# Expert layers of a routed MLP: two 64-token groups per step, one in each half of the array's columns, with both weight matrices streamed

## The chip, the cores and the metric

One core of one Trainium2 chip. The metric is device time in microseconds (us) of one execution, as the median of several runs. The profile and the trace are of one further execution of the same program, recorded by the hardware profiler.

## What is computed

Attention in chunks of 64 positions over 8 batches, 8 heads, 576 positions and head size 64. Its output, as 4608 tokens of 512 numbers, goes through 8 experts; each token goes to the one expert whose embedding is nearest by cosine.

```python
scores = scale * q_c @ k_c.T            # within each chunk of 64
x = softmax(scores) @ v_c               # -> (4608, 512)
logits = xn @ en.T / tau                # rows and expert embeddings normed
expert_idx = argmax(logits, axis=1)
out[mask] = gate_w[mask, None] * (relu(x[mask] @ w1[e]) @ w2[e])   # for each expert e
```

w1 is (8, 512, 1024) and w2 (8, 1024, 512), all in 32-bit floats. The inputs are drawn with a fixed seed, so the number of tokens of each expert can be worked out from the reference: 832, 359, 183, 448, 512, 1023, 576 and 675.

## The kernel before

It has three stages, and the order of all work is as written in the code (`manual_schedule`): each engine and each DMA queue takes its instructions in that order and waits where it must.

**Attention** (lines 88 to 267) goes through 36 tiles of 128 tokens. `load_qk` (L90) and `load_v` (L104) put the loads of q, k and v on SyncE's queue (SP), q and k three tiles ahead. Per tile, TensorE transposes k and q (`turn_qk`, L126), multiplies them in quarters of the array (`scores`, L144: 64 rows by 64 columns, four neighbours in the loop `for par: for c:` lie in four different quarters, and the two values of `c` lie in the same rows and in different columns), transposes the weights (L171) and multiplies by v, again in quarters (`values`, L184). `turn_x` (L208) and `logits` (L216) make the router's logits. The tile's rows go to DRAM on GpSimd's queue (L199). Beside it `load_w1` (L115) puts one piece of 512 KB of w1 per tile on SP, 32 pieces, so that all of w1 (16 MB) lies in `w1_sb` when the experts begin.

**Routing** (lines 279 to 432) is a chain of small VectorE operations: the best expert of each token, the token's rank among its expert's tokens, the number of blocks of each expert (L349), the first block of each (L352), the expert of each block (`eblk`, L358 to L366) and whether it differs from that two blocks before (`fresh`, L367, L368), each token's block and row (L380 to L382), its gate, and the token at each place by one-hot products (L404 to L430).

**Experts** (lines 437 to 566): 43 blocks of 128 tokens of one expert, the most that 4608 tokens and 8 experts can need. A block is gathered from DRAM by an indirect DMA on GpSimd (`gather`, L469, four ahead), transposed (`turn_xb`, L483), multiplied by w1 (`hidden`, L495), transposed again (`turn_h`, L516), multiplied by w2 (`result`, L527) and scattered (L536). `load_w2` (L459) puts a load of 2 MB into one of two buffers; it is skipped where that buffer holds the expert already. SP and TensorE read the block's expert into a register first (`number`, L450). A matrix product of 32-bit floats shows as two instructions, with a weight load before each, so `hidden` and `result` have 16 each. The loop runs, for step j:

```python
hidden(j + 1); turn_h(j); turn_xb(j + 2); result(j - 1); load_w2(j + 1); gather(j + XBUF)
```

Of the kernel before, what the change touches and what calls it, by code (L numbers as in the profile page):

```python
# [9 lines left out]
FP32 = mybir.dt.float32  # L10
# [8 lines left out]
P = 128  # L19
CH = 64  # L20
ROUND = 12582912.0  # 1.5 * 2**23: adding and subtracting it rounds to a whole number
# [4 lines left out]
def kernel(  # L26
# [17 lines left out]
    KD = D // P  # 128-row pieces of the model dimension  # L44
    KF = F // P  # 128-row pieces of the hidden dimension
    NT = N // P  # tiles of 128 tokens
    NCB = S // CH  # chunks in a batch
    NBLK = NT + E - 1  # blocks of 128 tokens of one expert, at most
# [6 lines left out]

    w1_sb = keep.tile([P, E, KD, F], FP32, name="w1_sb")
    w1_flat = w1_sb.rearrange("p e c f -> p (e c f)")
# [3 lines left out]
    src_row = keep.tile([P, NBLK], I32, name="src_row")  # L61
    dst_row = keep.tile([P, NBLK], I32, name="dst_row")
    gate_at = keep.tile([P, NBLK], FP32, name="gate_at")
    eblk = keep.tile([1, NBLK], I32, name="eblk")
    fresh = keep.tile([1, NBLK], I32, name="fresh")

    make_identity(nc, ident)

    # ------------------------------------------------------------------
    # chunk attention: x rows to DRAM, logits and squared norms on chip  # L70
    # ------------------------------------------------------------------
    with (
# [31 lines left out]
        def load_v(b):  # L104
            # odd heads' keys in the upper half, where their transposed weights come out
            t = v_p.tile([P, NPAIR, NCB, Dh], FP32, tag="v", name="v")
            for h in range(H):
                r0 = CH * (h % 2)
                nc.sync.dma_start(
                    out=t[r0 : r0 + CH, h // 2],  # L110
                    in_=v[b, h].rearrange("(c k) d -> k c d", k=CH),
                )
            v_t[b] = t

        def load_w1(j):  # L115
            e, c = divmod(j, KD)
            nc.sync.dma_start(out=w1_sb[:, e, c], in_=moe_w1[e, c * P : c * P + P])
# [106 lines left out]
        def set_up_experts():  # L224
            # rows of emb / (norm + 1e-6) / tau, turned
            junk = one.tile([P, D], FP32, tag="junk", name="junk")
            nc.scalar.activation(junk[0:E], emb, AF.Square, accum_out=emb_sq)
            nc.scalar.activation(emb_n, emb_sq, AF.Sqrt)
            nc.vector.tensor_scalar(emb_n, emb_n, 1e-6, None, ALU.add)
            nc.vector.reciprocal(emb_n, emb_n)  # L230
            nc.vector.reciprocal(tau_sb, tau_sb)
            nc.vector.tensor_scalar(emb, emb, emb_n, tau_sb, ALU.mult, ALU.mult)
            ps = ps_t.tile([P, KD, P], FP32, tag="tr", name="tr")
            for c in range(KD):
                nc.tensor.transpose(ps[:, c, 0:E], emb[:, c * P : c * P + P], ident[0:E, 0:E])
            nc.vector.tensor_copy(enT, ps[:, :, 0:E])
# [11 lines left out]
        for t in range(NT + 1):  # L248
            if t < NT:
                turn_a(t)  # L250
            if t + 1 < NT:
                turn_qk(t + 1)
                scores(t + 1)
            if t > 0:
                turn_x(t - 1)
            if t < NT:
                values(t)
                if t + 4 < NT:
                    load_qk(t + 4)
                b = (2 * t + 2) // NCB + 1  # L260
                if b not in v_t and b < B:
                    load_v(b)
                if 1 <= t <= KD * E:
                    load_w1(t - 1)
            if t > 0:
                logits(t - 1)
        nc.vector.tensor_copy(lg, lg_ps)

    # ------------------------------------------------------------------
    # routing: the best expert and its gate for each token, and a place for  # L270
    # each token among blocks of 128 that belong to one expert each
    # (counts and 0/1 masks are whole numbers up to 128, exact in bf16)
    # ------------------------------------------------------------------
    with (
# [42 lines left out]
        # rank of each token among its expert's  # L317
# [26 lines left out]
        # blocks of each expert, and the first of them  # L344
# [3 lines left out]
        half = 0.5 - 0.5 / P  # L348
        nc.vector.tensor_scalar(nb, tot, 1.0 / P, half, ALU.mult, ALU.add)  # L349
        nc.vector.tensor_scalar(nb, nb, ROUND, ROUND, ALU.add, ALU.subtract)  # L350
        nc.vector.tensor_tensor_scan(first, carry[:, 0, 1 : E + 1], nb, 0.0, ALU.mult, ALU.add)
        nc.vector.tensor_tensor(first, first, nb, ALU.subtract)  # L352
        nc.vector.tensor_scalar(off, first, float(P), None, ALU.mult)

        # expert of each block, and whether its weights differ from those two blocks before
        e_of = sp.tile([1, NBLK], FP32, name="e_of")
        ge = sp.tile([1, NBLK, E], FP32, name="ge")
        nc.vector.tensor_tensor(  # L358
            ge,
            io[0:1, 0:NBLK].unsqueeze(2).to_broadcast([1, NBLK, E]),  # L360
            first[0:1].unsqueeze(1).to_broadcast([1, NBLK, E]),
            ALU.is_ge,
        )
        nc.vector.tensor_reduce(e_of, ge, axis=AX.X, op=ALU.add)
        nc.vector.tensor_scalar(e_of, e_of, -1.0, None, ALU.add)
        nc.vector.tensor_copy(eblk, e_of)  # L366
        nc.vector.memset(fresh[:, 0:2], 1)  # L367
        nc.vector.tensor_tensor(  # L368
            fresh[:, 2:NBLK], e_of[:, 2:NBLK], e_of[:, 0 : NBLK - 2], ALU.not_equal
        )  # L370

        # place of each token: block and row
# [7 lines left out]
        nc.vector.tensor_scalar(blk, dest, 1.0 / P, -half, ALU.mult, ALU.add)  # L380
        nc.vector.tensor_scalar(blk, blk, ROUND, ROUND, ALU.add, ALU.subtract)
        nc.vector.scalar_tensor_tensor(  # L382
            out=row, in0=blk, scalar=-float(P), in1=dest, op0=ALU.mult, op1=ALU.add
        )

        # gates
# [13 lines left out]
        # token and gate at each place: one-hot products  # L400
        SK = [P, NT, NBLK]
        bm = sp.tile(SK, FP32, name="bm")
        rr = sp.tile([P, NT, 2, NBLK], FP32, name="rr")
        nc.vector.tensor_tensor(  # L404
            bm,
            io[:, 0:NBLK].unsqueeze(1).to_broadcast(SK),
# [5 lines left out]
        inv = ps_r.tile([P, 2, NBLK], FP32, name="inv")  # L412
# [10 lines left out]
        # an empty place reads row 0 and writes nowhere  # L423
        bad = sp.tile([P, NBLK], FP32, name="bad")
        tk = sp.tile([P, NBLK], FP32, name="tk")
# [8 lines left out]
    # ------------------------------------------------------------------  # L434
    # experts, a block of 128 tokens at a time
    # ------------------------------------------------------------------
    XBUF = 4
    with (
        tc.tile_pool(name="w2", bufs=1) as w2_p,
# [6 lines left out]
        w2_sb = [w2_p.tile([P, KF, D], FP32, name=f"w2_{i}") for i in range(2)]  # L446
        w2_rows = moe_w2.rearrange("e (c p) d -> p (e c) d", p=P)
# [10 lines left out]

        def load_w2(j):  # L459
            e = number(eblk[0:1, j : j + 1], E - 1, ENG.SP)  # L460
            # skipped where this buffer holds that expert already
            how = {}
            if j >= 2:
                how["cond"] = number(fresh[0:1, j : j + 1], 1, ENG.SP) > 0
            nc.sync.dma_start(out=w2_sb[j % 2], in_=w2_rows[:, ds(e * KF, KF), :], **how)

# [21 lines left out]
        def hidden(j):  # L488
            d = mo[j]
            e = number(eblk[0:1, j : j + 1], E - 1, ENG.PE)  # L490
            h = bp.tile([P, F], FP32, tag="h", name="h")
            for fh in range(F // 512):
                ps = ps_h.tile([P, 512], FP32, tag="h", name="h_ps")
                for c in range(KD):
                    nc.tensor.matmul(  # L495
                        ps,
                        lhsT=d["xT"][:, c],
                        rhs=w1_flat[:, ds(e * (KD * F) + c * F + fh * 512, 512)],
                        start=(c == 0),
                        stop=(c == KD - 1),  # L500
                    )
# [21 lines left out]
        def result(j):  # L523
            d = mo.pop(j)
            ps = ps_y.tile([P, D], FP32, tag="y", name="y_ps")
            for c in range(KF):
                nc.tensor.matmul(  # L527
                    ps,
                    lhsT=d["hT"][:, c],
                    rhs=w2_sb[j % 2][:, c],  # L530
                    start=(c == 0),
                    stop=(c == KF - 1),
                )
# [12 lines left out]

        load_w2(0)
# [4 lines left out]
        hidden(0)  # L552
        turn_xb(1)
        for j in range(NBLK + 1):
            if j + 1 < NBLK:
                hidden(j + 1)
            if j < NBLK:
                turn_h(j)
            if j + 2 < NBLK:
                turn_xb(j + 2)  # L560
            if j > 0:
                result(j - 1)
                if j + 1 < NBLK:
                    load_w2(j + 1)
            if j + XBUF < NBLK:
                gather(j + XBUF)
# [28 lines left out]
```

## Time and profile before

| | before |
|---|---|
| median of 3 runs | 1083.26 us (1082.6 to 1084.11) |
| span of the profiled execution | 1082.1 us |
| TensorE busy, matrix products | 940.4 us (87%) |
| VectorE, ScalarE, GpSimd busy | 272.5, 178.6, 109.7 us |
| bytes moved by DMA | 109.65 MB |

The profiled execution has no other time of its own than its span, which is 1.2 us under the median. PE is TensorE's matrix products, PEld its weight loads (they run beside the products), DVE is VectorE, ACT ScalarE, POOL GpSimd, SP SyncE. Starts are recorded; the ends of matrix products are modelled, so the time from one start to the next says more than a duration. The granted clock of TensorE is given as a share of 2.4 GHz; its two levels are 0.5 (1.2 GHz) and 1.0.

### The profile page before, as it was taken

What the parts mean: (1) busy time and instruction counts of PE and PEld (TensorE: products, weight loads), DVE (VectorE), ACT (ScalarE), POOL (GpSimd) and SP (SyncE); (2) the same over time, 40 slices, a digit from 0 to 9 for tenths busy, and PEclk for the clock granted to TensorE, in tenths of its full rate; (3) what the DMA queues carried; (4) which work ended last, traced back from release to release, by engine and by line L of the source; (5) the groups of instructions that cost most, each with busy time, mean ns of one, the idle gap of its engine ahead of it and who ended that gap; (6) DMA issues with size and microseconds to landing.
All of it is one profiled execution on the core that took longest, in us unless ns stands there. A gap on an engine that the chain in (4) does not pass through costs nothing.

```text
span 1082.1 us, 12876 instructions
## 1 busy us (share of the span) xinstructions
PE 940.4 (87%) x5139; PEld 569.7 (53%) x5139; DVE 272.5 (25%) x506; ACT 178.6 (17%) x319; POOL 109.7 (10%) x134
## 2 busy tenths in 40 slices
PE   4777777777777736999999999999999999999998
PEld 3666566666666624444444444444444444444443
DVE  3434434434434382111111111111111111111110
ACT  3222222222222210111111111111111110111101
POOL 0000000000000001011101111011110111101101
PEclk9999655555555555999999999999999999999999
DMA  9574755737744105011143531415100331321100
GB/s 189 143 171 130 178 143 156 181 113 180 167 129 116 40 0 204 1 39 40 47 162 117 193 111 44 165 40 194 39 30 29 117 117 39 120 89 39 40 3 0
DMA packets 144026, 109.65 MB, mean 101 GB/s; under 512 B 116118, under 2 KB 116118, under 8 KB 143968
## 3 DMA queue, kind: packets, MB, share of 16 engines
q1 hardware_dynamic: 134144, 78.66, 27.7%
q0 software_dynamic: 9824, 30.17, 7.8%
q8 instruction: 42, 0.69, 0.3%
q14 instruction: 16, 0.13, 0.0%
HBM read 146.55 MB, written 20.71 MB: 155 GB/s over the span
## 4 chain that ended last, share of the span: by engine, by line
issue 56%; PE 20%; DVE 14%; POOL 5%; ACT 2%; DMA 1%; POOLq 0%; SPq 0%
PE lg_ps L216 6%; PE tr L126 6%; PE sc L144 4%; POOL xin L469 4%; PE tr L171 3%; DVE a L154 2%; DVE mx L152 2%; DVE qT L131 2%; DVE rs L162 2%; ACT a L160 2%; DVE xT L210 2%; POOL out_dram L536 2%; PE inv L416 1%; DMA xin<-x_rows,src_row 1%; DVE rs L163 1%
## 5 line engine op out<-in xcount | busy, mean ns | idle before, releaser
L495 PE MATMUL h_ps<-w_sb,xbT 128*128 x688 | 304.9, 596 | 2.4 <-DVE xbT L485 1.6
L527 PE MATMUL y_ps<-w,hT 128*128 128x512 f32 x688 | 302.2, 592 | 0.0
L495 PEld LDWEIGHTS h_ps<-w_sb,xbT 128*128 128x128 f32 x688 | 131.4, 191 | 167.7 <-issue 164.5
L527 PEld LDWEIGHTS y_ps<-w,hT 128*128 128x128 f32 x688 | 127.5, 190 | 144.4 <-issue 144.4
L506 DVE TENSOR_SCALAR h<-h_ps 128x512 f32<-128x512 f32 x43 | 29.7, 691 | 400.6 <-PE h_ps L495 400.6
L216 PE MATMUL lg_ps<-enT,xT 128*128 128x8 f32 x288 | 64.2, 352 | 62.1 <-DVE xT L210 62.1
L536 POOL DMA_INDIRECT out_dram<-y,dst_row x43 | 43.5, 1011 | 558.9 <-ACT y L535 544.7
L216 PEld LDWEIGHTS lg_ps<-enT,xT 128*128 128x128 f32 x288 | 60.8, 312 | 69.0 <-DVE xT L210 68.9
L535 ACT ACTIVATE y<-y_ps,gate_at 128x512 f32<-128x512 f32 x43 | 29.5, 687 | 285.8 <-PE y_ps L527 285.8
L504 ACT ACTIVATE h<-h_ps 128x512 f32<-128x512 f32 x43 | 25.7, 597 | 308.3 <-PE h_ps L495 308.3
L144 PE MATMUL sc<-kT,qT 64*64 64x64 f32 x1152 | 40.8, 317 | 31.5 <-DVE qT L131 31.5
L520 DVE COPY hT<-ht_ps 128x512 f32<-128x512 f32 x43 | 29.7, 691 | 140.4 <-PE ht_ps L516 140.4
L131 DVE COPY qT<-tr 128x512 f32<-128x512 f32 x36 | 24.9, 691 | 139.2 <-PE tr L126 139.2
L144 PEld LDWEIGHTS sc<-kT,qT 64*64 64x64 f32 x1152 | 35.1, 218 | 44.9 <-issue 41.1
L199 POOL DMA_DIRECT2D x_rows<-x x36 | 19.5, 542 | 353.6 <-DVE x L192 353.6
L516 PEld LDWEIGHTS ht_ps<-ident,h 128*128 128x128 f32 x344 | 40.3, 141 | 22.7 <-issue 22.7
L469 POOL DMA_INDIRECT xin<-x_rows,src_row x43 | 43.9, 1021 | 52.4 <-DVE dst_row L430 35.1
L516 PE MATMUL ht_ps<-ident,h 128*128 128x128 f32 x344 | 44.6, 273 | 0.0
L160 ACT ACTIVATE a<-a 128x512 f32<-128x512 f32 x36 | 22.7, 629 | 132.5 <-DVE a L154 132.5
L126 PE MATMUL tr<-ident,kx 128*128 128x128 f32 x144 | 36.9, 409 | 6.0 <-DMA kx<-in_k_dram 6.0
L184 PE MATMUL sc<-v,aT 64*64 64x64 f32 x1152 | 40.8, 318 | 0.2 <-ACT aT L173 0.2
L184 PEld LDWEIGHTS sc<-v,aT 64*64 64x64 f32 x1152 | 34.1, 218 | 11.8 <-issue 11.3
(108 smaller groups left out, 615.3 us busy)
## 6 DMA issues: line engine op xcount, KB each, us to landing
w<-in_moe_w_dram SPq DMA_DIRECT2D x43, 2048.0 KB
w_sb<-in_moe_w_dram SPq DMA_DIRECT2D x32, 512.0 KB
v<-in_v_dram SPq DMA_DIRECT2D x64, 144.0 KB
x_rows<-x POOLq DMA_DIRECT2D x36, 256.0 KB, 2.3
qx<-in_q_dram SPq DMA_DIRECT2D x32, 256.0 KB
kx<-in_k_dram SPq DMA_DIRECT2D x32, 256.0 KB
qx<-in_q_dram SPq DMA_DIRECT2D x8, 128.0 KB
kx<-in_k_dram SPq DMA_DIRECT2D x8, 128.0 KB
```

Source lines behind the costliest of these rows:

```text
L126: nc.tensor.transpose(ps[:, i], a[:, i * P : i * P + P], ident)
L131: nc.vector.tensor_copy(x, ps)
L144: nc.tensor.matmul(sc[CH * c : CH * c + CH, par, i], lhsT=qx[r0 : r0 + CH, i, c0 : c0 + CH], rhs=kx[r0 : r0 + CH, i, c0 : c0 + CH], start= ...
L160: nc.scalar.activation(a, a, AF.Exp, scale=scale)
L171: nc.tensor.transpose(ps[:, i], d["a"][:, i].rearrange("p r k -> p (r k)"), ident)
L184: nc.tensor.matmul(pv[CH * c : CH * c + CH, par, i], lhsT=d["aT"][r0 : r0 + CH, i, CH * c : CH * c + CH], rhs=v_t[b][r0 : r0 + CH, i, cb], ...
L216: nc.tensor.matmul(lg_ps[:, t], lhsT=d["xT"][:, c], rhs=enT[:, c], start=(c == 0), stop=(c == KD - 1),)
L469: nc.gpsimd.indirect_dma_start(out=t, out_offset=None, in_=x_rows, in_offset=bass.IndirectOffsetOnAxis(ap=src_row[:, j : j + 1], axis=0), ...
L495: nc.tensor.matmul(ps, lhsT=d["xT"][:, c], rhs=w1_flat[:, ds(e * (KD * F) + c * F + fh * 512, 512)], start=(c == 0), stop=(c == KD - 1),)
L516: nc.tensor.transpose(ps[:, c], d["h"][:, f0 : f0 + P], ident)
L527: nc.tensor.matmul(ps, lhsT=d["hT"][:, c], rhs=w2_sb[j % 2][:, c], start=(c == 0), stop=(c == KF - 1),)
L536: ins = nc.gpsimd.indirect_dma_start(out=out, out_offset=bass.IndirectOffsetOnAxis(ap=dst_row[:, j : j + 1], axis=0), in_=y, in_offset=Non ...
```

## The change

The experts' work is cut into groups of 64 tokens (G) instead of blocks of 128, and a step takes two groups: one from the front of the list of groups, in the lower 64 columns of the array, one from its back, in the upper 64. `NST` is 40 steps. The two groups of a step may belong to different experts, so each half has its own weights: two buffers of w1 and two of w2 per half, 2 MB each. w1 no longer stays on the chip whole. In attention, the buffers of the first two steps are filled with the first expert's weights (front) and the last one's (back), 8 loads of 2 MB at every fourth tile; during the experts, both w1 and w2 are loaded anew into a buffer whose expert changes. TensorE reads no register any more; SP reads two per half and step. The transposes stay as they were.

```diff
+    w1_sb = [[keep.tile([P, KD, F], FP32, name=f"w1_{s}{i}") for i in range(2)] for s in range(2)]
+    w2_sb = [[keep.tile([P, KF, D], FP32, name=f"w2_{s}{i}") for i in range(2)] for s in range(2)]
...
-                if 1 <= t <= KD * E:
-                    load_w1(t - 1)
+                if t % 4 == 3 and t // 4 < 8:
+                    load_first(t // 4)
...
-        nc.vector.tensor_scalar(nb, tot, 1.0 / P, half, ALU.mult, ALU.add)
+        nc.vector.tensor_scalar(nb, tot, 1.0 / G, half, ALU.mult, ALU.add)
+        nc.vector.tensor_scalar(ngm1, first[:, E - 1 : E], -1.0, None, ALU.add)
+        nc.vector.tensor_scalar(mid, first[:, E - 1 : E], 0.5, 0.25, ALU.mult, ALU.add)
+        nc.vector.tensor_scalar(mid, mid, ROUND, ROUND, ALU.add, ALU.subtract)
...
+        nc.vector.tensor_copy(jj[:, 0], io[0:1, 0:NST])
+        nc.vector.tensor_scalar(jj[:, 1], io[0:1, 0:NST], -1.0, ngm1[0:1], ALU.mult, ALU.add)
...
-        nc.vector.memset(fresh[:, 0:2], 1)
+        for i in range(2):
+            nc.vector.tensor_scalar(
+                fresh[:, i, 0:2], e_of[:, i, 0:2], float((0, E - 1)[i]), None, ALU.not_equal
+            )
...
+        nc.vector.tensor_scalar(back, blk, mid, None, ALU.is_ge)
+        nc.vector.scalar_tensor_tensor(
+            out=row, in0=back, scalar=float(G), in1=row, op0=ALU.mult, op1=ALU.add
+        )
+        nc.vector.tensor_scalar(turn, blk, -2.0, ngm1, ALU.mult, ALU.add)
+        nc.vector.tensor_tensor(turn, turn, back, ALU.mult)
+        nc.vector.tensor_tensor(blk, blk, turn, ALU.add)
...
+        def load_w(buf, rows, n, s, j):
+            if (s, j) not in new:
+                new[s, j] = (
+                    number(eblk[0:1, s, j : j + 1], E - 1, ENG.SP),
+                    number(fresh[0:1, s, j : j + 1], 1, ENG.SP),
+                )
+            e, f = new[s, j]
+            nc.sync.dma_start(out=buf[s][j % 2], in_=rows[:, ds(e * n, n), :], cond=f > 0)
...
                 for c in range(KD):
-                    nc.tensor.matmul(
-                        ps,
-                        lhsT=d["xT"][:, c],
-                        rhs=w1_flat[:, ds(e * (KD * F) + c * F + fh * 512, 512)],
...
+                    for s in range(2):
+                        nc.tensor.matmul(
+                            ps[G * s : G * s + G],
+                            lhsT=d["xT"][:, c, G * s : G * s + G],
+                            rhs=w1_sb[s][j % 2][:, c, fh * 512 : fh * 512 + 512],
...
+        load_w1(0)
+        load_w1(1)
         load_w2(0)
         load_w2(1)
...
-        for j in range(NBLK + 1):
-            if j + 1 < NBLK:
+        for j in range(NST + 1):
+            if j + 1 < NST:
                 hidden(j + 1)
+                if j + 3 < NST:
+                    load_w1(j + 3)
```

`result` is changed as `hidden` is, with `w2_sb[s][j % 2][:, c]`; `load_w1(j)` and `load_w2(j)` call `load_w` for both halves. Where both do their work, the order on SP in step j is `load_w1(j + 3)` and then `load_w2(j + 1)`.

## Rows read from the trace of the kernel before

**Rows 1.** Busy time by stage; columns: stretch, its length, then as headed.
```profile
core 0: us, PE busy (x) PEld busy (x) DVE busy (x) ACT busy (x) POOL busy (x), PEclk, DMA share, GB/s
0.00:380.00 380.00, 273.33 (x3172) 237.05 (x3172) 155.96 (x294) 95.14 (x187) 21.61 (x45) 0.67 0.60 145
380.00:424.30 44.30, 16.33 (x75) 15.67 (x75) 27.44 (x84) 3.08 (x4) 4.80 (x8) 0.50 0.16 56
424.30:1082.10 657.80, 650.73 (x1892) 316.94 (x1892) 89.12 (x129) 80.38 (x129) 83.27 (x82) 0.99 0.23 79
```

**Rows 2.** TensorE's own waits in the experts' stage; us in total, times, longest.
```profile
PE x_ps L483 <- DMA xin<-x_rows,src_row: 9.8, 1, 9.8
PE h_ps L495 <- DVE xbT L485: 1.6, 2, 0.8
PE h_ps L495 <- DMA w<-in_moe_w_dram: 0.8, 1, 0.8
```

**Rows 3.** Timeline of TensorE over one step; start, length, instructions (x count).
```profile
506.40 7.03 PE L495 MATMUL h_ps<-w_sb,xbT 128*128 x16
513.27 1.04 PE L516 MATMUL ht_ps<-ident,h 128*128 128x128 f32 x8
514.14 0.60 PE L483 MATMUL x_ps<-ident,xin 128*128 128x128 f32 x4
514.58 7.03 PE L527 MATMUL y_ps<-w,hT 128*128 128x512 f32 x16
521.45 0.59 PE L495 MATMUL h_ps<-w_sb,xbT 128*128 x1
```

**Rows 4.** Timeline of TensorE over part of one attention tile.
```profile
290.03 1.06 PE L126 MATMUL tr<-ident,kx 128*128 128x128 f32 x4
290.88 1.06 PE L126 MATMUL tr<-ident,qx 128*128 128x128 f32 x4
...
293.89 1.11 PE L208 MATMUL tr<-ident,x 128*128 128x128 f32 x4
294.93 0.39 PE L184 MATMUL sc<-v,aT 64*64 64x64 f32 x4
```

**Rows 5.** The same tile's scores, cut at 293.16 us.
```profile
292.82 0.60 PE L144 MATMUL sc<-kT,qT 64*64 64x64 f32 x12 [0.88 <-DVE qT L131]
```

**Rows 6.** Weight loads of both expert products, from the groups of instructions.
```profile
L495 PEld LDWEIGHTS h_ps<-w_sb,xbT 128*128 128x128 f32 x688 | 131.4, 191 | 167.7 <-issue 164.5
L527 PEld LDWEIGHTS y_ps<-w,hT 128*128 128x128 f32 x688 | 127.5, 190 | 144.4 <-issue 144.4
```

**Rows 7.** VectorE in the routing, groups of instructions.
```profile
L358 DVE TENSOR_TENSOR ge<-io,first 1x344 f32<-1x344 f32 x1 | 0.5, 496 | 0.0
L364 DVE TENSOR_REDUCE e_of<-ge 1x43 f32<-1x344 f32 x1 | 0.5, 499 | 0.0
L382 DVE SCALAR_TENSOR_TENSOR row<-blk,dest 128x36 f32<-128x36 f32 x1 | 0.2, 195 | 0.0
L353 DVE TENSOR_SCALAR off<-first 128x8 f32<-128x8 f32 x1 | 0.2, 172 | 0.0
```

**Rows 8.** The chain that ended last: start, length, what (the first gather).
```profile
415.87 8.34 DMA xin<-x_rows,src_row
```

**Rows 9.** DMA: issues, count, median us to landing; and SP's queue in bytes.
```profile
xin<-x_rows,src_row POOLq DMA_INDIRECT x43, 3.9
q1 hardware_dynamic: 134144, 78.66, 27.7%
```

**Rows 10.** Stretches with w2 loads; the last two columns are DMA share and GB/s.
```profile
416.60:432.00 15.40, 6.87 (x12) 3.27 (x13) 0.69 (x1) 0.00 (x0) 4.38 (x5) 0.54 0.97 351
583.00:592.00 9.00, 9.00 (x32) 4.65 (x31) 2.07 (x3) 1.18 (x2) 1.84 (x2) 1.00 0.88 289
```

**Rows 11.** SP's register reads, and its longest waits in the whole span and in attention.
```profile
L451 SPq TENSOR_LOAD <-fresh x41: 261/266/273, 417.3 to 1048.7; - x41
...
SPq L465 <- PE y_ps L527: 586.5, 41, 33.6
...
SPq L97 <- PE tr L126: 182.2, 24, 8.7
```

More of the change, by code (lines that the diff above doesn't have):

```diff
@@ L47 @@
     NCB = S // CH
-    NBLK = NT + E - 1
+    G = P // 2
+    NST = NT + E // 2
     scale = 1.0 / float(Dh) ** 0.5
@@ L54 @@
     ctx.enter_context(tc.manual_schedule())
-    w1_sb = keep.tile([P, E, KD, F], FP32, name="w1_sb")
-    w1_flat = w1_sb.rearrange("p e c f -> p (e c f)")
+    w1_sb = [[keep.tile([P, KD, F], FP32, name=f"w1_{s}{i}") for i in range(2)] for s in range(2)]
+    w2_sb = [[keep.tile([P, KF, D], FP32, name=f"w2_{s}{i}") for i in range(2)] for s in range(2)]
+    w1_rows = moe_w1.rearrange("e (c p) f -> p (e c) f", p=P)
+    w2_rows = moe_w2.rearrange("e (c p) d -> p (e c) d", p=P)
     ident = keep.tile([P, P], FP32, name="ident")
@@ L60 @@
     nsq = keep.tile([P, NT], FP32, name="nsq")
[L61 to L65, printed above, removed]
+    src_row = keep.tile([P, NST], I32, name="src_row")
+    dst_row = keep.tile([P, NST], I32, name="dst_row")
+    gate_at = keep.tile([P, NST], FP32, name="gate_at")
+    eblk = keep.tile([1, 2, NST], I32, name="eblk")
+    fresh = keep.tile([1, 2, NST], I32, name="fresh")
     make_identity(nc, ident)
@@ L113, in load_v, with load_first @@
             v_t[b] = t
-        def load_w1(j):
-            e, c = divmod(j, KD)
-            nc.sync.dma_start(out=w1_sb[:, e, c], in_=moe_w1[e, c * P : c * P + P])
+        def load_first(n):
+            kind, rest = divmod(n, 4)
+            i, s = divmod(rest, 2)
+            e = (0, E - 1)[s]
+            if kind:
+                nc.sync.dma_start(out=w2_sb[s][i], in_=w2_rows[:, e * KF : e * KF + KF, :])
+            else:
+                nc.sync.dma_start(out=w1_sb[s][i], in_=w1_rows[:, e * KD : e * KD + KD, :])
         qT, kT = {}, {}
@@ L347 @@
         off = sp.tile([P, E], FP32, name="off")
-        half = 0.5 - 0.5 / P
-        nc.vector.tensor_scalar(nb, tot, 1.0 / P, half, ALU.mult, ALU.add)
+        ngm1 = sp.tile([P, 1], FP32, name="ngm1")
+        mid = sp.tile([P, 1], FP32, name="mid")
+        half = 0.5 - 0.5 / G
+        nc.vector.tensor_scalar(nb, tot, 1.0 / G, half, ALU.mult, ALU.add)
         nc.vector.tensor_scalar(nb, nb, ROUND, ROUND, ALU.add, ALU.subtract)
         nc.vector.tensor_tensor_scan(first, carry[:, 0, 1 : E + 1], nb, 0.0, ALU.mult, ALU.add)
+        nc.vector.tensor_scalar(ngm1, first[:, E - 1 : E], -1.0, None, ALU.add)
@@ L352 @@
+        nc.vector.tensor_scalar(mid, first[:, E - 1 : E], 0.5, 0.25, ALU.mult, ALU.add)
+        nc.vector.tensor_scalar(mid, mid, ROUND, ROUND, ALU.add, ALU.subtract)
         nc.vector.tensor_tensor(first, first, nb, ALU.subtract)
-        nc.vector.tensor_scalar(off, first, float(P), None, ALU.mult)
-        e_of = sp.tile([1, NBLK], FP32, name="e_of")
-        ge = sp.tile([1, NBLK, E], FP32, name="ge")
+        nc.vector.tensor_scalar(off, first, float(G), None, ALU.mult)
+        JE = [1, 2 * NST, E]
@@ L358 @@
+        e_of = sp.tile([1, 2, NST], FP32, name="e_of")
+        jj = sp.tile([1, 2, NST], FP32, name="jj")
+        ge = sp.tile(JE, FP32, name="ge")
+        nc.vector.tensor_copy(jj[:, 0], io[0:1, 0:NST])
+        nc.vector.tensor_scalar(jj[:, 1], io[0:1, 0:NST], -1.0, ngm1[0:1], ALU.mult, ALU.add)
         nc.vector.tensor_tensor(
             ge,
-            io[0:1, 0:NBLK].unsqueeze(2).to_broadcast([1, NBLK, E]),
-            first[0:1].unsqueeze(1).to_broadcast([1, NBLK, E]),
+            jj.rearrange("p s j -> p (s j)").unsqueeze(2).to_broadcast(JE),
+            first[0:1].unsqueeze(1).to_broadcast(JE),
@@ L362 @@
             ALU.is_ge,
         )
-        nc.vector.tensor_reduce(e_of, ge, axis=AX.X, op=ALU.add)
+        nc.vector.tensor_reduce(
+            e_of.rearrange("p s j -> p (s j)"), ge, axis=AX.X, op=ALU.add
+        )
         nc.vector.tensor_scalar(e_of, e_of, -1.0, None, ALU.add)
         nc.vector.tensor_copy(eblk, e_of)
-        nc.vector.memset(fresh[:, 0:2], 1)
+        for i in range(2):
+            nc.vector.tensor_scalar(
+                fresh[:, i, 0:2], e_of[:, i, 0:2], float((0, E - 1)[i]), None, ALU.not_equal
+            )
@@ L368 @@
         nc.vector.tensor_tensor(
-            fresh[:, 2:NBLK], e_of[:, 2:NBLK], e_of[:, 0 : NBLK - 2], ALU.not_equal
+            fresh[:, :, 2:NST], e_of[:, :, 2:NST], e_of[:, :, 0 : NST - 2], ALU.not_equal
         )
@@ L379 @@
         nc.vector.tensor_reduce(dest, w.rearrange("p e s -> p s e"), axis=AX.X, op=ALU.add)
-        nc.vector.tensor_scalar(blk, dest, 1.0 / P, -half, ALU.mult, ALU.add)
+        back = sp.tile([P, NT], FP32, name="back")
+        turn = sp.tile([P, NT], FP32, name="turn")
+        nc.vector.tensor_scalar(blk, dest, 1.0 / G, -half, ALU.mult, ALU.add)
         nc.vector.tensor_scalar(blk, blk, ROUND, ROUND, ALU.add, ALU.subtract)
         nc.vector.scalar_tensor_tensor(
-            out=row, in0=blk, scalar=-float(P), in1=dest, op0=ALU.mult, op1=ALU.add
+            out=row, in0=blk, scalar=-float(G), in1=dest, op0=ALU.mult, op1=ALU.add
         )
+        nc.vector.tensor_scalar(back, blk, mid, None, ALU.is_ge)
[5 more added lines that the diff above has]
+        nc.vector.tensor_tensor(blk, blk, turn, ALU.add)
         rn = sp.tile([P, NT], FP32, name="rn")
@@ L398 @@
         nc.vector.reciprocal(gate, gate)
-        SK = [P, NT, NBLK]
+        SK = [P, NT, NST]
         bm = sp.tile(SK, FP32, name="bm")
-        rr = sp.tile([P, NT, 2, NBLK], FP32, name="rr")
+        rr = sp.tile([P, NT, 2, NST], FP32, name="rr")
         nc.vector.tensor_tensor(
             bm,
-            io[:, 0:NBLK].unsqueeze(1).to_broadcast(SK),
+            io[:, 0:NST].unsqueeze(1).to_broadcast(SK),
             blk.unsqueeze(2).to_broadcast(SK),
@@ L411 @@
         nc.vector.tensor_tensor(rr[:, :, 1], bm, gate.unsqueeze(2).to_broadcast(SK), ALU.mult)
-        inv = ps_r.tile([P, 2, NBLK], FP32, name="inv")
+        inv = ps_r.tile([P, 2, NST], FP32, name="inv")
         for s in range(NT):
@@ L422 @@
             )
-        bad = sp.tile([P, NBLK], FP32, name="bad")
-        tk = sp.tile([P, NBLK], FP32, name="tk")
+        bad = sp.tile([P, NST], FP32, name="bad")
+        tk = sp.tile([P, NST], FP32, name="tk")
         nc.vector.tensor_copy(tk, inv[:, 0])
@@ L438 @@
     with (
-        tc.tile_pool(name="w2", bufs=1) as w2_p,
         tc.tile_pool(name="blk", bufs=2) as bp,
@@ L445 @@
     ):
-        w2_sb = [w2_p.tile([P, KF, D], FP32, name=f"w2_{i}") for i in range(2)]
-        w2_rows = moe_w2.rearrange("e (c p) d -> p (e c) d", p=P)
         xin, mo = {}, {}
@@ L457, in number, with load_w1 @@
             )
-        def load_w2(j):
[L460 to L465, printed above, removed]
+        new = {}
+        def load_w(buf, rows, n, s, j):
[3 more added lines that the diff above has]
+                    number(fresh[0:1, s, j : j + 1], 1, ENG.SP),
+                )
+            e, f = new[s, j]
+            nc.sync.dma_start(out=buf[s][j % 2], in_=rows[:, ds(e * n, n), :], cond=f > 0)
+        def load_w1(j):
+            for s in range(2):
+                load_w(w1_sb, w1_rows, KD, s, j)
+        def load_w2(j):
+            for s in range(2):
+                load_w(w2_sb, w2_rows, KF, s, j)
+                del new[s, j]
         def gather(j):
@@ L489, in hidden @@
             d = mo[j]
-            e = number(eblk[0:1, j : j + 1], E - 1, ENG.PE)
             h = bp.tile([P, F], FP32, tag="h", name="h")
@@ L494, in hidden @@
                 for c in range(KD):
-                    nc.tensor.matmul(
-                        ps,
-                        lhsT=d["xT"][:, c],
-                        rhs=w1_flat[:, ds(e * (KD * F) + c * F + fh * 512, 512)],
-                        start=(c == 0),
-                        stop=(c == KD - 1),
-                    )
+                    for s in range(2):
+                        nc.tensor.matmul(
+                            ps[G * s : G * s + G],
+                            lhsT=d["xT"][:, c, G * s : G * s + G],
+                            rhs=w1_sb[s][j % 2][:, c, fh * 512 : fh * 512 + 512],
+                            start=(c == 0),
+                            stop=(c == KD - 1),
+                        )
                 dst = h[:, fh * 512 : fh * 512 + 512]
@@ L526, in result @@
             for c in range(KF):
[L527 to L533, printed above, removed]
+                for s in range(2):
+                    nc.tensor.matmul(
+                        ps[G * s : G * s + G],
+                        lhsT=d["hT"][:, c, G * s : G * s + G],
+                        rhs=w2_sb[s][j % 2][:, c],
+                        start=(c == 0),
+                        stop=(c == KF - 1),
+                    )
             y = bp.tile([P, D], FP32, tag="y", name="y", bufs=3)
@@ L552 @@
         hidden(0)
+        load_w1(2)
         turn_xb(1)
-        for j in range(NBLK + 1):
-            if j + 1 < NBLK:
+        for j in range(NST + 1):
+            if j + 1 < NST:
                 hidden(j + 1)
-            if j < NBLK:
+                if j + 3 < NST:
+                    load_w1(j + 3)
+            if j < NST:
                 turn_h(j)
-            if j + 2 < NBLK:
+            if j + 2 < NST:
                 turn_xb(j + 2)
@@ L562 @@
                 result(j - 1)
-                if j + 1 < NBLK:
+                if j + 1 < NST:
                     load_w2(j + 1)
-            if j + XBUF < NBLK:
+            if j + XBUF < NST:
                 gather(j + XBUF)
```

## The prediction, made before the changed kernel was run

> **What bounds the kernel now.** I read the busy time by stage first [rows 1]: attention takes 380 us, routing and the first gather 44, and the experts 657.8 us, in which TensorE's products are busy for 650.7 at the upper clock level (0.99 granted). Then TensorE's own waits in that stage [rows 2]: 12.2 us in all, 9.8 of it for the first gather. So the experts' stage is a queue of TensorE work and nothing else, and its length is the number of blocks times the time of one. The timeline of one block [rows 3] gives that time: from one start of L495 to the next, 521.45 - 506.40 = 15.05 us. Of it `hidden` takes 513.27 - 506.40 = 6.87 us for 16 instructions (0.43 each), the 12 transposes 1.31, `result` 6.87. 43 blocks are 647 us.
>
> **The change, part by part**
>
> *Three steps fewer.* 40 steps of 15.05 us are 602 us: -45.2 us, if a step of two half-wide groups costs what a block of 128 did. From the token counts there are 13 + 6 + 3 + 7 + 8 + 16 + 9 + 11 = 73 groups of 64, so 40 steps of two hold them all.
>
> *Do the halves run side by side?* Each product becomes two, of 64 columns each and with the same 512 columns streamed, so a step issues 64 instructions where 32 stood. Nothing in the experts' stage shows such a pair; attention does, at the lower clock. There a 128-column transpose takes (290.88 - 290.03) / 4 = 0.213 us [rows 4], so 64 streamed columns are some 0.107 us. The first twelve instructions of the scores start within 0.34 us [rows 5], that is, four in each 0.107 us, and all 32 leave room for the next work at 293.89, 1.07 us after the first start, where one after the other they would need 32 x 0.107 = 3.4. Neighbours there share rows and differ in columns, with different streams, which is just the pair of the change. What differs is the clock (0.5 against 1.0), 128 rows instead of 64, and 512 columns. Bounds: full overlap (0 us) and none (40 x 13.74 = +550). I take full overlap, since the nearest row shows four at a time. If the two passes of a product held up the neighbour, the second half would trail by one pass, 0.43 us a step: +17, kept for the range.
>
> *Weight loads.* There are 64 per step, each of half the columns. At the old length, 0.191 us, two fit into one 0.43 us product [rows 6]. Cost 0.
>
> *Switches between half-wide and full-wide work.* Now every product of a step has the full width. After the change, each step goes from halves (`hidden`) to full (12 transposes) and back to halves (`result`; the next `hidden` follows it in halves). Attention shows the price at the lower clock: the 32 scores need 8 x 0.107 = 0.853 us and take 1.07, so 0.22 more before the transposes; these need 0.853 and take 294.93 - 293.89 = 1.04, so 0.19 more before the next quarters [rows 4, 5]. About 0.2 us per switch. If it were all array cycles, the upper clock would halve it to 0.1. No row shows it there; the bounds are 0 and 0.2, so 0 to 16 us over 80 switches. I take 0.13, nearer the half: +10.4 us.
>
> *Routing.* New on the path are some ten operations of 0.17 to 0.20 us (`ngm1`, `mid` twice, two for `jj`, five for `back`, `row`, `turn`, `blk`), two small ones in place of a memset, and `ge` and `e_of` over 640 numbers instead of 344, +0.4 each at 496 and 499 ns [rows 7]. `bm` and `rr` shrink by 40/43. Together +2.5 us, on VectorE's chain that releases the first gather.
>
> *The first gather.* Before, it goes out with two 2 MB loads of w2 on SP, and 8.34 us pass until it lands [rows 8]; the median of all gathers is 3.9 [rows 9]. After, the first experts' weights come during attention: experts 0 and 7 fill at least two groups each, so the conditional loads for steps 0 and 1 are all skipped. -4.4 us.
>
> *Weights streamed beside the experts.* From the counts, the front half changes expert at steps 13, 19, 22, 29 and 37, the back half at 11, 20 and 36; each change reloads both buffers of both layers, 4 x 2.1 MB. That is 32 loads in this stage where 16 stood, so SP's queue moves 78.7 + 33.5 = 112 MB [rows 9]. w1 for step j goes out at the end of `hidden(j - 2)` and is due at `hidden(j)`, a good 23 us later; w2 for step j likewise between results. The tight place is steps 16 to 22, with 12 loads in 7 steps of 15.3 us (107 us). With DMA saturated, 351 GB/s were moved; a load with the gather and the scatter beside it took the 9.0 us of the second stretch [rows 10]. At the first rate, 12 x 2.1 + 7 x 0.52 = 28.8 MB take 82 us, and nothing is late. At 9.0 us a load it is 108 us, and walking through the deadlines leaves about 5 us of waits. I take 1 and keep 0 to 6 for the range.
>
> *SP's queue.* Each step adds two register reads per half, 4 x 0.27 us, and four loads to be issued or skipped, some 4 us of the 15 [rows 11]; w1 is put ahead of w2 on this queue, and waits for `hidden` while `result` isn't over anyway. SP waits 586 us for `result` today, which is the cover. In attention, 2 MB bursts replace 512 KB pieces ahead of q and k; those go out as soon as a buffer is free (SP waits 182 us for L126), three tiles or 31 us before use, and a burst takes 7 to 9 us: 0. If that cover went, each of 8 bursts could cost up to 8 us. TensorE's register reads lay beside its products: 0. DVE, ACT and GpSimd do three steps less of the same, hidden.
>
> *Sum.* -45.2 + 10.4 + 2.5 - 4.4 + 1 = -35.7. From the span of 1082.1 that is 1046.4; with the 1.2 us by which the median stands above it, **1047.6 us**.
>
> **Rivals**
>
> *A: the halves overlap only in part.* This is the case on the other side. Without its price the change gains some 36 us, 0.9 per step; so it turns slower once the products of a step take 13.74 + 0.9, 6.6% more than in full width. For it: no row shows two streams over 128 rows at the upper clock, and a limit on what the array can be fed would show first there. Against it: four at a time in attention, at no loss beyond the switches [rows 5]. The Trainium skill's page "TensorE: Matmul & The Clock Gate", in "Measured speedup vs the span model", gives 2.38x for three packed column tiles, where full overlap would be 3x; no run here shows it. By that share (0.79) the products of a step would take 17.3 us, which as an estimate from that page makes the kernel about 1190 us. Without the page: half the overlap lost is 40 x 6.9 = +275, so 1320, none at all 1600. Chance 0.09.
>
> *B: the clock falls.* Attention stands at a mean of 0.67 and its quarter-wide products run at the lower level, though TensorE is busy for 72% of it [rows 1]; if products in halves, or the gaps at the switches, do not hold the upper level, a step takes up to twice as long, 1600 us. Against it: the experts' stage leaves no gaps, and the change puts in about 2% of them. Chance 0.03.
>
> *C: the weights come late.* If loads share the DMA engines worse than today, at 10 us each, the waits at steps 19 to 23 and 36 to 38 add 15 us (1063); with q and k late in attention as well, 1075. Still faster. Against it: the saturated stretch [rows 10]. Chance 0.10.
>
> **How the numbers follow.** Forecast 0.76 and C 0.10 are faster, A and B 0.12 slower, and 0.02 for a mix of A and C that lands at no change (within 0.2%, 2.2 us, about what a measurement of this kernel can tell). Faster 0.86, same 0.02, slower 0.12. The low end has free switches and no waits: 1047.6 - 11.4 = 1036. The high end takes switches at 0.2 (+6), waits of 6 (+5) and half of the trailing pass (+9): 1068, which takes in most of C. A and B lie outside, so about 0.17 is left out.
>
> **What would show it.** From one `hidden` to the next 15.2 to 15.5 us, with 32 instructions in about 6.9 us; gaps of 0.1 to 0.2 us before the transposes and before `result`; the first gather landing some 4 us after its issue; about 112 MB on SP's queue; TensorE waiting for w1 or w2 only around steps 20 to 23, if at all; clock near 1.0 in the whole stage. Steps of 17 us and more without waits would make the prediction wrong by A, a clock of 0.5 in the experts by B, waits for w1 and w2 of over 10 us by C.

## The result, and the profile after

The changed kernel takes 1047.05 us (median of 4 runs, 1045.62 to 1047.5) against 1083.05 for the kernel before (4 runs, one more than in the table ahead): a ratio of 0.9666, 95% interval 0.9652 to 0.9679. The profiled execution has a span of 1045.6 us, 36.5 less than before.

Busy time by stage of the changed kernel, cut at the end of attention and at the first transpose of the experts:

```profile
core 0: us, PE busy (x) PEld busy (x) DVE busy (x) ACT busy (x) POOL busy (x), PEclk, DMA share, GB/s
0.00:378.50 378.50, 273.21 (x3172) 236.91 (x3172) 155.81 (x293) 94.96 (x186) 21.59 (x44) 0.57 0.53 145
378.50:420.70 42.20, 16.36 (x76) 15.68 (x75) 29.62 (x95) 3.24 (x4) 3.77 (x7) 0.50 0.04 8
420.70:1045.60 624.90, 618.00 (x3040) 232.70 (x3040) 83.02 (x120) 74.91 (x120) 78.56 (x78) 0.99 0.39 140
```

Against [rows 1], the experts' stage went from 657.8 to 624.9 us. Its shape is the same: TensorE busy nearly throughout, the clock at the upper level (0.99). What it moves by DMA went from 79 to 140 GB/s.

Timeline of TensorE over one step:

```profile
566.13 7.04 PE L541 MATMUL h_ps<-w,xbT 128*64 128x512 f32 x32
573.09 1.09 PE L562 MATMUL ht_ps<-ident,h 128*128 128x128 f32 x8
574.02 0.60 PE L529 MATMUL x_ps<-ident,xin 128*128 128x128 f32 x4
574.55 7.09 PE L574 MATMUL y_ps<-w,hT 128*64 128x512 f32 x32
581.47 7.04 PE L541 MATMUL h_ps<-w,xbT 128*64 128x512 f32 x32
```

The step is 581.47 - 566.13 = 15.34 us, where [rows 3] had 15.05. Twice the instructions, 32 of half the columns, fit into 6.96 us where 16 took 6.87: the halves run side by side. The 0.29 us more are spread over the ends of the three parts: `hidden` +0.09, the 12 transposes 1.46 instead of 1.31, `result` +0.05.

TensorE's own waits in the stage, the first gather and SP's queue:

```profile
PE x_ps L529 <- DMA xin<-x_rows,src_row: 5.3, 1, 5.3
PE h_ps L541 <- DVE xbT L531: 2.4, 3, 0.8
```

```profile
417.12 1.11 POOL L515 DMA_INDIRECT xin<-x_rows,src_row  x1 [37.59 <-DVE dst_row L465]
```

```profile
q1 hardware_dynamic: 144256, 112.21, 34.6%
HBM read 391.14 MB, written 19.92 MB: 393 GB/s over the span
```

There is no wait for w1 or w2 [rows 2]. The first gather is issued at 417.12, and its block's transposes begin at 420.75 (end of the 5.3 us wait): 3.6 us, where 8.3 to 8.5 passed before [rows 8]. SP's queue moved 112.2 MB, as worked out.

### The profile page after: what moved, and what is told of

It is laid out like the page before. It is cut to its first block, busy times and chain, and to the rows that moved or that the text cites. A ratio compares the mean times of both kernels' runs of the same rounds, so it can differ in the third digit from the quotient of the medians.

```text
span 1045.6 us, 15287 instructions
## 1 busy us (share of the span) xinstructions
PE 907.6 (87%) x6287; PEld 485.3 (46%) x6287; DVE 268.5 (26%) x508; ACT 173.1 (17%) x310; POOL 103.9 (10%) x128
## 3 DMA queue, kind: packets, MB, share of 16 engines
HBM read 391.14 MB, written 19.92 MB: 393 GB/s over the span
## 4 chain that ended last, share of the span: by engine, by line
issue 56%; PE 21%; DVE 14%; POOL 5%; ACT 2%; POOLq 0%; DMA 0%; SPq 0%
PE lg_ps L226 6%; PE tr L136 6%; PE sc L154 4%; POOL xin L515 4%; PE tr L181 3%; DVE mx L162 2%; DVE a L164 2%; DVE qT L141 2%; DVE rs L172 2%; ACT a L170 2%; DVE xT L220 2%; POOL out_dram L583 2%; PE inv L451 1%; DVE rs L173 1%; DMA kx<-in_k_dram 0%
## 5 line engine op out<-in xcount | busy, mean ns | idle before, releaser
L541 PE MATMUL h_ps<-w,xbT 128*64 128x512 f32 x1280 | 284.5, 597 | 2.4 <-DVE xbT L531 2.4
L574 PE MATMUL y_ps<-w,hT 128*64 128x512 f32 x1280 | 283.3, 595 | 0.0
L541 PEld LDWEIGHTS h_ps<-w,xbT 128*64 128x64 f32 x1280 | 92.3, 138 | 186.5 <-issue 183.3
L574 PEld LDWEIGHTS y_ps<-w,hT 128*64 128x64 f32 x1280 | 88.5, 137 | 167.0 <-issue 167.0
L583 POOL DMA_INDIRECT out_dram<-y,dst_row x40 | 40.6, 1014 | 532.6 <-ACT y L582 517.2
L582 ACT ACTIVATE y<-y_ps,gate_at 128x512 f32<-128x512 f32 x40 | 27.5, 688 | 272.9 <-PE y_ps L574 272.9
L562 PEld LDWEIGHTS ht_ps<-ident,h 128*128 128x128 f32 x320 | 34.3, 140 | 32.5 <-issue 32.5
L515 POOL DMA_INDIRECT xin<-x_rows,src_row x40 | 41.0, 1024 | 49.5 <-DVE dst_row L465 37.6
L218 PE MATMUL tr<-ident,x 128*128 128x128 f32 x144 | 40.0, 433 | 0.0
```

The source lines that it names most:

```text
L218: nc.tensor.transpose(ps[:, c], d["x"][:, c * P : c * P + P], ident)
L515: nc.gpsimd.indirect_dma_start(out=t, out_offset=None, in_=x_rows, in_offset=bass.IndirectOffsetOnAxis(ap=src_row[:, j : j + 1], axis=0), ...
L541: nc.tensor.matmul(ps[G * s : G * s + G], lhsT=d["xT"][:, c, G * s : G * s + G], rhs=w1_sb[s][j % 2][:, c, fh * 512 : fh * 512 + 512], sta ...
L562: nc.tensor.transpose(ps[:, c], d["h"][:, f0 : f0 + P], ident)
L574: nc.tensor.matmul(ps[G * s : G * s + G], lhsT=d["hT"][:, c, G * s : G * s + G], rhs=w2_sb[s][j % 2][:, c], start=(c == 0), stop=(c == KF ...
L583: ins = nc.gpsimd.indirect_dma_start(out=out, out_offset=bass.IndirectOffsetOnAxis(ap=dst_row[:, j : j + 1], axis=0), in_=y, in_offset=Non ...
```

## The experiments

**1. The halves in turn: is it the alternation that makes them overlap?**

```diff
-                for c in range(KD):
-                    for s in range(2):
+                for s in range(2):
+                    for c in range(KD):
```

The same in `result`.

> All products of the front half, then all of the back half, within each accumulation. Theory (two halves run side by side only where their instructions alternate): the halves run one after the other but for the one instruction at each of 6 changes of half in a step, so a step's products take 27.4 - 6 x 0.43 = 24.8 us instead of 13.8, and the run some 1047 + 40 x 11 = 1490 us. Rival (TensorE looks far enough ahead, or keeps a queue per half): 1047 us, step 15.34.

Measured: 1266.86 us (one run), between the two. Timeline of TensorE around the change from one `result` (L574) to the next `hidden` (L541):

```profile
621.25 1.09 PE L562 MATMUL ht_ps<-ident,h 128*128 128x128 f32 x8
...
622.71 11.00 PE L574 MATMUL y_ps<-w,hT 128*64 128x512 f32 x29
633.12 0.64 PE L541 MATMUL h_ps<-w,xbT 128*64 128x512 f32 x1
633.54 0.59 PE L574 MATMUL y_ps<-w,hT 128*64 128x512 f32 x1
633.60 0.59 PE L541 MATMUL h_ps<-w,xbT 128*64 128x512 f32 x1
633.97 0.59 PE L574 MATMUL y_ps<-w,hT 128*64 128x512 f32 x1
634.03 0.59 PE L541 MATMUL h_ps<-w,xbT 128*64 128x512 f32 x1
634.40 0.59 PE L574 MATMUL y_ps<-w,hT 128*64 128x512 f32 x1
634.46 7.63 PE L541 MATMUL h_ps<-w,xbT 128*64 128x512 f32 x29
642.02 1.09 PE L562 MATMUL ht_ps<-ident,h 128*128 128x128 f32 x8
```

The front half of the next product begins at 633.12, beside the last passes of the back half: three more of them still start after it, at 633.54, 633.97 and 634.40. So work of the other half is not held until the queue reaches it in order; it starts while some four passes of the first half are still to be done. The step is 20.77 us (621.25 to 642.02, transposes to transposes), 5.4 more than with alternation, not 11: the theory had the direction, and its size was wrong since it let one pass overlap per change of half. With four the sum comes out. A step has five such changes, not six: three in `hidden`, one in `result`, one between `result` and the next `hidden`. Then 20 of the 64 passes run beside another, and the other 44, of 0.43 us each, take 18.9 us; each change adds some 0.06 (633.54 to 633.60), and with 1.46 for the transposes and the 0.14 that the changed kernel pays at the ends of its products this is 20.8. In `result` itself 29 passes start within 10.4 us (622.71 to 633.12), which is 24 times 0.43 and not 28: four of them had a partner. So the partial overlap that rival A foresaw does exist; what brings it here is the order of the instructions, and no limit on what the array can be fed shows.

**2. The halves in turn after two products.** This tests what the first run suggested. The loop over c goes in twos: two products of the front half, two of the back.

```diff
-                for c in range(KD):
-                    for s in range(2):
+                for c, s in ((c + i, s) for c in range(0, KD, 2) for s in range(2) for i in range(2)):
```

> The halves take turns after two products (four passes) instead of one. Theory (as the run with the halves in turn suggests, the other half's work starts while up to four passes of the first are still to be done): full overlap, 1047 us. Rival (work of the other half starts only beside the last pass of a run): a round of 8 passes takes 7 x 0.43 instead of 4, 1047 + 40 x 10 = 1450 us or, with what the halves in turn showed per change, over 1100.

Measured: 1047.96 us (two runs), ratio 0.9684 (0.9666 to 0.9702). Timeline from one step's transposes to the next:

```profile
573.69 1.09 PE L562 MATMUL ht_ps<-ident,h 128*128 128x128 f32 x8
...
589.08 1.09 PE L562 MATMUL ht_ps<-ident,h 128*128 128x128 f32 x8
```

The step is 15.39 us, 0.05 more than with single products. Runs of four passes cost next to nothing, as four passes of look-ahead would have it; runs of 8 and 16 (experiment 1) cost 5.4 us a step.

**3. Full width again, everything else as changed: are the 0.29 us the switches?**

```diff
-                    for s in range(2):
-                        nc.tensor.matmul(
-                            ps[G * s : G * s + G],
-                            lhsT=d["xT"][:, c, G * s : G * s + G],
-                            rhs=w1_sb[s][j % 2][:, c, fh * 512 : fh * 512 + 512],
+                    nc.tensor.matmul(
+                        ps,
+                        lhsT=d["xT"][:, c],
+                        rhs=w1_sb[c % 2][j % 2][:, c, fh * 512 : fh * 512 + 512],
```

> Products in the full width of 128 columns again, with the same 40 steps, loads, buffers and routing (the weights of the two halves alternate over c, so the output is not that of the experts: both halves of a step are multiplied by a mix of the two experts' weights). Theory (the 0.29 us that a step gained are two switches of width): the step falls from 15.34 to 15.05 us and the run to 1047 - 40 x 0.29 = 1035.4 us. Rival (the 0.29 us come from the loads or buffers beside it): 1047 us.

Measured: 1034.17 us, ratio 0.9557 (0.9542 to 0.9572). Timeline of one step:

```profile
560.61 7.03 PE L540 MATMUL h_ps<-w,xbT 128*128 128x512 f32 x16
567.48 1.04 PE L561 MATMUL ht_ps<-ident,h 128*128 128x128 f32 x8
...
568.79 7.03 PE L572 MATMUL y_ps<-w,hT 128*128 128x512 f32 x16
575.65 7.03 PE L540 MATMUL h_ps<-w,xbT 128*128 128x512 f32 x16
```

The step is 15.04 us again with the same loads beside it. The whole of the 0.29 us belongs to working in halves between full-wide transposes, none of it to the loads. Full width also halves the number of instructions and weight loads; experiment 7 tells these from the switches.

**4. w1 loaded anew in every step: how near is the limit of DMA?**

```diff
-            nc.sync.dma_start(out=buf[s][j % 2], in_=rows[:, ds(e * n, n), :], cond=f > 0)
+            how = {} if n == KD and j >= 2 else {"cond": f > 0}
+            nc.sync.dma_start(out=buf[s][j % 2], in_=rows[:, ds(e * n, n), :], **how)
```

> w1 is loaded anew in every step from 2 on, for both halves, expert changed or not: 76 + 16 = 92 loads of 2.1 MB instead of 32, with gathers and scatters 214 MB in the experts' stage. Theory (loads share some 350 GB/s): 610 us of transfers in a stage of 622, so TensorE waits only around the changes of expert, 1055 to 1080 us. Rival (9.0 us a load, as the lone loads of before): 828 us of transfers, 1250 to 1270 us.

Measured: 1053.04 us (one run), 6 more than the changed kernel and just under the range that was expected. Busy time from 450 to 1045 us, TensorE's waits for weights, the transposes of two successive steps, and bytes:

```profile
450.00:1045.00 595.00, 593.62 (x2919) 223.41 (x2920) 78.18 (x113) 72.43 (x116) 75.21 (x74) 1.00 0.90 344
```

```profile
PE h_ps L542 <- DMA w<-in_moe_w_dram: 2.7, 4, 1.4
```

```profile
773.74 1.09 PE L563 MATMUL ht_ps<-ident,h 128*128 128x128 f32 x8
...
790.60 1.09 PE L563 MATMUL ht_ps<-ident,h 128*128 128x128 f32 x8
```

```profile
q1 hardware_dynamic: 175936, 238.04, 64.2%
HBM read 391.14 MB, written 19.92 MB: 391 GB/s over the span
```

344 GB/s were moved for 595 us on end, and the row of waits for weights has 2.7 us. By the steps' lengths the weights cost more, since this row leaves out time that the modelled ends of products cover: four steps in a row, around the changes of expert, take 16.5 to 16.9 us (790.60 - 773.74 = 16.86) instead of 15.34, and the first is 2.5 longer, together 8 us. A load costs its share of that rate, not the 9.0 us of a lone load; the changed kernel, with a third of these loads, is far from the limit.

**5. The loads for steps 0 and 1 not skipped: is that why the first gather is early?**

```diff
-        for i in range(2):
-            nc.vector.tensor_scalar(
-                fresh[:, i, 0:2], e_of[:, i, 0:2], float((0, E - 1)[i]), None, ALU.not_equal
-            )
+        nc.vector.memset(fresh[:, :, 0:2], 1)
```

> The loads for steps 0 and 1 are not skipped: 8 loads of 2.1 MB go out on SP as soon as the routing has the experts, at about 390 us, and at 350 GB/s last until about 438. Theory (the first gather lands early because nothing shares the DMA engines with it): it takes 8.3 us again instead of 3.5, w1 of step 0 is there by then, +4.8: 1052 us. Rival (the gather is early for another reason): 1047 us.

Measured: 1047.46 us (1046.94 to 1049.5), ratio 0.9687 (0.9672 to 0.9703): no difference that the runs can tell. The first gather in the chain that ended last, and busy time while it is under way:

```profile
414.94 6.18 DMA xin<-x_rows,src_row
```

```profile
417.00:421.00 4.00, 0.00 (x0) 0.00 (x0) 0.00 (x0) 0.00 (x0) 2.36 (x3) 0.50 1.05 395
```

The DMA engines are full (395 GB/s), and the gather takes 6.2 us instead of 3.6. So sharing does lengthen it, by 2.6 of the 4.8 expected; in the profiled run the attention before it happened to end 2.0 us earlier, and the time from the first transposes of x to those of h was 0.8 shorter (both vary between runs, see below), and the sum vanished. That the loads cost the gather time is shown; that they made up all of the 4.8 us is not.

**6. 37 steps instead of 40.** `NST = NT + 1`.

> 37 steps instead of 40: enough for the 73 groups of these inputs, not for every routing. Theory (an empty step costs what a full one does, 15.34 us): 1047 - 46 = 1001 us, or a little less for smaller routing tables. Rival (the last steps are partly hidden in the tail): over 1010 us.

Measured: 1009.45 us, ratio 0.9331 (0.9317 to 0.9345): 37.6 less than the changed kernel by the medians and 36 by the two ratios, not 46. The end of both kernels, first the 37 steps (the last transposes of h, TensorE's last products, the last scatter, busy time behind it, and the instruction DRAIN with which GpSimd ends the program), then the changed kernel:

```profile
976.26 1.09 PE L562 MATMUL ht_ps<-ident,h 128*128 128x128 f32 x8
...
986.43 7.08 PE L574 MATMUL y_ps<-w,hT 128*64 128x512 f32 x30 [1.21 <-DMA w<-in_moe_w_dram]
...
994.56 0.98 POOL L583 DMA_INDIRECT out_dram<-y,dst_row  x1 [8.20 <-ACT y L582]
```

```profile
994.56:997.00 2.44, 0.00 (x0) 0.00 (x0) 0.00 (x0) 0.00 (x0) 0.98 (x1) 1.00 0.14 54
997.00:1005.60 8.60, 0.00 (x0) 0.00 (x0) 0.00 (x0) 0.00 (x0) 0.00 (x0) 0.52 0.00 0
L642 POOLq DRAIN  x3: 51/99/10436, 994.3 to 1005.3; - x3
```

```profile
1026.12 1.09 PE L562 MATMUL ht_ps<-ident,h 128*128 128x128 f32 x8
...
1042.16 0.98 POOL L583 DMA_INDIRECT out_dram<-y,dst_row  x1 [5.93 <-ACT y L582]
```

```profile
L642 POOLq DRAIN  x3: 51/99/2766, 1041.9 to 1045.4; - x3
```

From the issue of the last scatter to the end of the span it is 11.0 us here (1005.6 - 994.56) and 3.4 in the changed kernel (1045.6 - 1042.16), whose last three steps are empty and scatter nothing. It is not the scatter's data that takes so long: the 64 rows of the last step's front half (its back half is empty) have been moved by 997.0, 54 GB/s for 2.44 us, and nothing moves after that. What lasts is GpSimd's DRAIN, 10.4 us (10436 ns) here and 2.8 there. Why it lasts longer behind a scatter that writes rows is not shown. The wait for the weights of the last step comes on top: from the last transposes of h to the last scatter 18.3 us pass here and 16.0 there. So the three empty steps cost 46 us and cover 7.6 + 2.3 us at the end, which leaves the 36 of the ratios. It is no version to keep: other inputs can need up to 79 groups.

**7. Two steps in one round: half the switches.** `hidden` of two steps, then 24 transposes, then `result` of two steps; h has four buffers.

```diff
+            for j in (a + 2, a + 3):
+                if j < NST:
+                    hidden(j)
...
+            for j in (a, a + 1):
+                turn_h(j)
+                if j + 4 < NST:
+                    turn_xb(j + 4)
+            for j in (a, a + 1):
+                result(j)
```

> Two steps in one round: both hidden, then all 24 transposes, then both results, so that there are two switches of width in two steps instead of four. Theory (a switch costs some 0.145 us, whatever stands between): 20 x 0.29 = -5.8, 1041 us. Rival (the transposes of two steps in a row wait for PSUM to be emptied, some 0.3 us or more a round): 1047 us or slower.

Measured: 1044.32 us, ratio 0.9648 (0.9635 to 0.9661). Timeline of TensorE's transposes in one round:

```profile
575.27 1.09 PE L562 MATMUL ht_ps<-ident,h 128*128 128x128 f32 x8
576.20 0.60 PE L529 MATMUL x_ps<-ident,xin 128*128 128x128 f32 x4
576.76 1.09 PE L562 MATMUL ht_ps<-ident,h 128*128 128x128 f32 x8
577.69 0.60 PE L529 MATMUL x_ps<-ident,xin 128*128 128x128 f32 x4
578.22 13.95 PE L574 MATMUL y_ps<-w,hT 128*64 128x512 f32 x64
```

A round is 30.57 us against 2 x 15.34 = 30.68. Four transposes take 0.44, so the third line should start at 576.64; it starts at 576.76, and the 8 transposes take 0.93 instead of 0.87. Both were right in part: the switches went, and waits for a PSUM buffer took some two thirds of what that gave. The products of a round take 30.57 - 2.95 = 27.62 us (2.95 from 575.27 to 578.22); two steps of full width have 4 x 6.87 = 27.48, two of the changed kernel 2 x 13.88 = 27.76. With half the switches half of the excess is left, at the same number of instructions and weight loads, so it goes with the switches.

**8. The same with PSUM buffers moved,** beside the changed kernel on one chip: `ps_h` two buffers instead of three, `ps_ht` three instead of two.

> Two steps in one round, with three PSUM buffers for the transposes of h and two for the hidden layer instead of two and three. Theory (in the first version of the pairs the second group of transposes waited 0.18 us a round for a PSUM buffer, and the rest of the saving was there): 30.36 to 30.45 us a round instead of 30.57, so another 20 x 0.12 to 0.2 = -2.4 to -4, and about 5 us below the changed kernel, 1042. Rival (the wait moves to the next buffer, that of x): 30.57 a round, 1044.

> The changed kernel once more, on the same chip as the next run: 1047 us.

Measured: 1042.75 us, ratio 0.9643 (0.963 to 0.9656), and the changed kernel once more 1046.07, ratio 0.9676 (0.9663 to 0.969). The same stretch:

```profile
576.77 1.09 PE L562 MATMUL ht_ps<-ident,h 128*128 128x128 f32 x8
577.70 0.60 PE L529 MATMUL x_ps<-ident,xin 128*128 128x128 f32 x4
578.13 1.04 PE L562 MATMUL ht_ps<-ident,h 128*128 128x128 f32 x8
579.08 0.66 PE L529 MATMUL x_ps<-ident,xin 128*128 128x128 f32 x4
579.67 13.95 PE L574 MATMUL y_ps<-w,hT 128*64 128x512 f32 x64
```

The wait before the third line is gone (578.13 - 577.70 = 0.43), and a shorter one stands before the fourth (0.95 for 8 transposes): the buffer of x, as the rival said. A round is 30.52 us, 0.05 less than in experiment 7 where 0.12 to 0.2 were expected: of the two accounts the rival's is the nearer. This version beats both kernels, the changed one by 3.3 us, and 20 rounds that are 0.16 us shorter than two of its steps make 3.2 of them.

## Why the prediction was right, point by point

- **Three steps fewer, full overlap.** 40 x 15.05 us is what experiment 3 shows for full width, and the halves add 0.29 to that and no pass more. The value taken between the far bounds (0 and +550) was the right one, and the row it rested on, four starts in each 0.107 us at the lower clock [rows 5], carried over to 128 rows, 512 columns and the upper clock.
- **Switches.** Forecast 0.13 us each, 10.4 in all; measured 0.29 / 2 = 0.145, 11.6 in all. The lower clock's 0.2 us [rows 4, 5] became neither half nor whole of itself.
- **Routing.** Forecast +2.5. From the copy of the logits at the end of attention to the first gather's issue it is 415.87 - 379.81 = 36.1 us before and 417.12 - 378.57 = 38.6 after: +2.5.
- **The first gather.** Forecast -4.4; from its issue to the first transpose it is 424.35 - 415.87 = 8.5 us before and 3.6 after: -4.9. That the loads are the whole cause stays open (experiment 5).
- **Streamed weights.** Forecast +1 of 0 to 6; measured 0. Of the two rates offered, the saturated one decides (experiment 4): lone loads are no measure of what loads cost together.
- **SP's queue.** Forecast 0; in attention TensorE waits for a load only once in either kernel, for the first k, so the loads of 2 MB made no q, k or v late.
- **Not forecast:** attention ended 1.2 us earlier (the logits' copy at 378.57 instead of 379.81). Of this 1.1 lies ahead of TensorE's first product, in its wait for the first k:

```profile
PE tr L126 <- DMA kx<-in_k_dram: 6.0, 1, 6.0
PE tr L136 <- DMA kx<-in_k_dram: 4.9, 1, 4.9
```

  The first line is of the kernel before, the second of the changed one. What goes out ahead of this load is the same in both, so nothing that the change touches explains the difference; the kernel before has one profile, and the cause stays open. Over the profiled runs with the changed attention the logits' copy falls between 376.1 and 378.9 us. The start of the experts, from the first transposes of x to those of h, took 20.3 us instead of 19.5, at 0.81 and 0.83 granted; in the second profiled run of the changed kernel (experiment 8) it took 18.7, so this is scatter as far as the runs show.
- **The sum.** It hit to 0.8 us (-35.7 forecast, -36.5 in the profiled spans) since errors cancelled: switches +1.1 and the start +0.8 against attention -1.2, the weights -1.0 and the gather -0.5. The mechanism, three steps fewer at full overlap, was right; that the total came out within a microsecond was luck.
- **Rival A** did not occur at this order of instructions, though experiment 1 shows what it costs at another. The Trainium skill ("TensorE: Matmul & The Clock Gate", "Measured speedup vs the span model") has 2.38x for three column tiles (of 32 columns each, which no run here packs). Here 64 passes take 6.96 + 6.92 = 13.88 us where 64 of 0.43 us would take 27.5, which is 1.98x for two tiles of 64. The Trainium skill's 2.38 of 3, a share of 0.79, does not carry over to this pair. **Rival B** did not occur: 0.99 granted. **Rival C** did not: the changed kernel never waits for weights, and nearly three times its loads, at 344 GB/s, cost 8 us in all (experiment 4).

## What to carry to other kernels

A step that is bound by TensorE can be split into two half-wide streams with different operands at little cost (here 0.29 us on a step of 15.05), as long as the instructions of the halves take turns within a few passes and the full-wide work between them is gathered into few places; count the switches. For weights streamed beside the work, judge by the saturated rate of the DMA engines, not by the length of a lone load. Before empty steps at the end are cut, look at what their time covers.

## What the runs showed of the hardware that was not expected

- Work of the other column half starts while some four passes (two 32-bit products) of the first are still to be done: alternating by one or by two products costs nearly the same (15.34 and 15.39 us a step), alternating by 4 in `hidden` and 8 in `result` costs 220 us.
- At the end of the program GpSimd's DRAIN took 10.4 us behind a scatter of 64 rows, whose data had been moved 2.4 us after its issue, and 2.8 us behind one that wrote nothing (experiment 6; one profiled run of each, cause open).
- The profile page's line on HBM counts loads that were skipped: it says 391.14 MB both for the changed kernel, whose SP queue moved 112 MB, and for experiment 4, which moved 238; the queue's own line is the one to read.
